# A tuned kernel's first five microseconds: which queue carries Wq's first two quarters, when the first is issued, and how many zero blocks TensorE runs

## The chip, the cores and the metric

The kernel runs on one core of a Trainium2 chip. A core has a matrix engine (TensorE, PE in the profile, its weight loads PEld), a vector engine (VectorE, DVE), a scalar engine (ScalarE, ACT), GpSimd (POOL) and SyncE (SP). SP and ACT also issue DMA transfers, each through a queue of its own; the transfers are carried out by 16 DMA engines. Each engine takes its instructions in the order in which the program gives them, and waits on semaphores for what other engines or transfers have to deliver.

The metric is the device time of one execution in microseconds (us). Beside it stands a profiled execution, whose records show every instruction and transfer.

## What is computed

The input x has 2048 rows (positions) of 512 elements, in bf16. Two branches are computed and mixed by a gate:

```python
x = A_x
g = _sigmoid((x * gate_w).sum(-1, keepdims=True))
a = _A_ref(x, A_wqkv, A_wo)
b = _B_ref(x, B_w1, B_b1, B_w2, B_b2)
return g * a + (1 - g) * b
```

Branch A projects x to q, k and v with one 512 by 1536 matrix, 32 heads of 16 each. Every position attends to eight positions, itself and the seven before it at steps of two; softmax over these eight, the weighted sum of v, and a projection with Wo. Branch B normalizes each row of x, multiplies along the positions with w1 (2048 to 1792), adds b1, applies GELU, multiplies with w2 (1792 back to 2048) and adds b2.

## The kernel before, in words

Positions are laid out in 16 tiles of 128. The kernel first needs x transposed (channels on partitions) for the projections of q and k, so the first thing it builds is the transposed x of the first 512 positions, XT, whose four blocks of 128 channels are filled in two ways. Blocks 1 to 3 come by a transposing DMA (`ld_xt0`, L473). Block 0 is loaded untransposed (`d_xp`, L479) and transposed on TensorE by four matmuls against an identity matrix (`f_tr`, L545). ScalarE (L555) and VectorE (L557) copy the results out of PSUM.

Wq, 512 by 512, is loaded in four quarters of 128 rows and 128 KB (`ld_w(0, d, 1)`), Wk in two halves of 256 KB (`ld_w(1, d, 2)`). The first projections are made for 512 positions in six groups (L635): four matmuls with Wq's first quarter and channel block 0, four with the second quarter and block 1, and so on for the third and fourth, then eight with each half of Wk. All matmuls of the projections have the line L619. The first group therefore waits for block 0 and Wq's first quarter, and the second group for the transposing DMA and Wq's second quarter.

Before the first data arrive TensorE multiplies constants into a bank that nobody reads (`f_warm`, L537): six blocks of 512 columns, one of 256, and one of 512 behind the transposes. They keep the array busy and compute nothing that is used; the text calls them zero blocks, as the change's own words do.

After the projections TensorE runs, without a gap, the scores of the attention in two bursts (L698), the two large products of branch B (L812 and L862) and the output projection (L878). VectorE makes the products of q with shifted k (L690), the row statistics of branch B (L574), the softmax, the weighted sums of v (L797 to L802) and the final mixture (L899). ScalarE copies out of PSUM (L627, L630), normalizes (L598) and applies the nonlinear functions.

The order on each engine comes from a planner in the kernel file. Operations are added with what they read and write, an estimated duration and, for the first loads, an expected landing time (`lands`); the planner places them one by one and derives semaphore waits from the data they share. Some orders are given by hand (`order.add`, `chain`). The first loads have their own waits cleared (`op_.deps.clear()`, L489), so they are issued as early as their queue allows:

```python
first_loads = [ld_w(0, 0, 1, "act"), ld_xt0(), ld_w(0, 1, 1, "act"), ld_w(0, 2, 1), ld_w(0, 3, 1), ld_w(1, 0, 2), ld_w(1, 2, 2),
               ld_x(0, 2)]
```

On SP the order of issue is: the slice for block 0, the transposing DMA, Wq's third and fourth quarter, Wk's two halves, two tiles of x, the transposing DMA of the next 512 positions, and the rest. On ACT it is Wq's first and second quarter, then a load of the activation table, then the copy at L555. GpSimd writes constants, the identity matrix (L417) and some zeros (L420, L421, L518).

Of the kernel before, what the change touches and what calls it, by code (L numbers as in the profile page):

```python
# [333 lines left out]
def bass_gated_mix__sliding_local_dilated__mixer_token_mlp__prompt_kernel(nc, A_x, A_wqkv, A_wo, B_x, B_w1, B_b1, B_w2, B_b2, gate_w, out, dbg=None):  # L334
    with contextlib.ExitStack() as es:
# [75 lines left out]
        def psub(ap_, p0, np_, offs, dims):  # L411
# [3 lines left out]
        A = sch.add  # L415

        c_ident = A("pool", lambda e: e.affine_select(out=IDENT, in_=nc.const_aps.tensor(1.0, [128, 128], BF16), pattern=[[1, 128]], compare_op=ALU.is_equal,  # L417
                                                     fill=0.0, base=0, channel_multiplier=-1),
                    0.4, writes=["ident"], name="ident")
# [8 lines left out]
        def mk_dma(dst, src):  # L428
            return lambda e: e.dma_start(dst, src)
# [3 lines left out]
        def throttle():  # L433
            return [init_dmas[-5]] if len(init_dmas) >= 5 else []

        def prev_dma():
            return [init_dmas[-1]] if init_dmas else []

        def ld_x(t0, n, q="sp"):
            ds = sch.dsem("x%d" % t0)  # L440
            op = sch.dma(q, mk_dma(X[:, t0:t0 + n, :], xv[:, t0:t0 + n, :]), n * 128 * D * 2, ds,
                         writes=["x%d" % t for t in range(t0, t0 + n)], deps=throttle() if q == "sp" else [], after=prev_dma() if q == "sp" else [], name="d_x%d" % t0)
            if q == "sp":
                init_dmas.append(op)
            return op

        def ld_w(tn, d0, n, q="sp"):
            ds = sch.dsem("wqkv%d_%d" % (tn, d0))
            op = sch.dma(q, mk_dma(WQKV[:, d0:d0 + n, tn * D:(tn + 1) * D], wqkv_v[:, d0:d0 + n, tn * D:(tn + 1) * D]),
                         n * 128 * D * 2, ds, writes=["wqkv%d_%d" % (tn, dt) for dt in range(d0, d0 + n)],  # L450
                         deps=throttle() if q == "sp" and n == 4 else [], after=prev_dma() if q == "sp" else [],
                         issue=0.65 if n == 4 else 0.45, name="d_wp%d_%d" % (tn, d0))
            if q == "sp":
                init_dmas.append(op)
            return op
# [14 lines left out]
        def ld_xt0():  # L470
            ds = sch.dsem("xt0")
            dst = XT[:, 1:4, 0:512]
            op = sch.dma("sp", lambda e: e.dma_start_transpose(dst, x2d[0:512, 128:512]), 512 * 384 * 2, ds, issue=1.25,  # L473
                         writes=XT0[1:4], after=prev_dma(), name="d_xt0")
            init_dmas.append(op)
            return op

        XP = view("OUTS", BF16, [(128, 4), (1, 128)])
        d_xp = sch.dma("sp", mk_dma(XP, xv[:, 0:4, 0:128]), 512 * 128 * 2, sch.dsem("xp"), writes=["outs0"], issue=0.4, name="d_xp")  # L479
        d_xp.lands = 3.9  # L480
        init_dmas.append(d_xp)

        first_loads = [ld_w(0, 0, 1, "act"), ld_xt0(), ld_w(0, 1, 1, "act"), ld_w(0, 2, 1), ld_w(0, 3, 1), ld_w(1, 0, 2), ld_w(1, 2, 2),
                       ld_x(0, 2)]
        ld_xt(1)
        first_loads.append(init_dmas[-1])
        for op_, t_ in zip(first_loads, (3.5, 5.7, 5.0, 6.3, 6.7, 7.6, 8.6, 9.4, 11.0)):
            op_.lands = t_
            op_.deps.clear()  # L489
        first_loads[2].order.add(first_loads[0])  # L490
        init_dmas[:] = [first_loads[1]] + first_loads[5:]
        ld_x(2, 2)
        ld_x(4, 4)
# [7 lines left out]
        def ld_w1(j):  # L501
# [4 lines left out]
            if j < 4:  # L506
# [8 lines left out]
                       writes=["wo"], deps=throttle(), after=prev_dma(), name="d_wo")  # L515
# [4 lines left out]
        for i_, (v_, n_) in enumerate(((B_b1, NFT), (B_b2, NST))):  # L520
            vr = v_.rearrange("(t q j) -> q t j", q=4, j=32)
            for q_ in range(4):
                sch.dma("sp", mk_dma(psub(BR, 32 * q_, n_, 32 * i_, [(1, 32)]), vr[q_]), n_ * 64, ds_b, reads=["br"],
                        writes=["br_%d_%d" % (i_, q_)], deps=throttle(), after=prev_dma(), name="d_b_%d_%d" % (i_, q_), issue=0.45)
        d_w1.append(ld_w1(3))
        A("dve", lambda e: e.transpose(out=BT, in_=BR), 0.2, reads=["br_%d_%d" % (i_, q_) for i_ in range(2) for q_ in range(4)],
          writes=["btc"], name="t_b")
# [5 lines left out]
        def f_warm(n, w_=D):  # L533
            def fn(e):
                ins = None
                for _ in range(n):
                    ins = e.matmul(ps[:, 7, 0:w_], lhsT=CONE[:, 0:128], rhs=CONE[:, 0:w_], start=True, stop=True)  # L537
                return ins
            return fn

        def f_tr(h):
            def fn(e):
                ins = None
                for t in range(2):
                    ins = e.matmul(ps[:, 5 + h, 128 * t:128 * t + 128], lhsT=XP[:, 2 * h + t, :], rhs=IDENT, start=True, stop=True)  # L545
                return ins
            return fn

        A("pe", f_warm(6), 2.56, writes=["lg7_0", "lg7_1"], name="warm1", prio=-100)
        w2_ = A("pe", f_warm(1, 256), 0.2, writes=["lg7_0", "lg7_1"], name="warm2", prio=-100)  # L550
        ta_ = A("pe", f_tr(0), 0.215, reads=["outs0", "ident"], writes=["lg5_0", "lg5_1"], after=[w2_], name="tr0", prio=-100)
        tr_ = A("pe", f_tr(1), 0.215, reads=["outs0", "ident"], writes=["lg6_0", "lg6_1"], after=[ta_], name="tr1", prio=-100)
        A("pe", f_warm(1), 0.43, writes=["lg7_0", "lg7_1"], after=[tr_], name="warm3", prio=-100)
# [2 lines left out]
          writes=["xt0_0"], name="ev_tra", prio=0)  # L556
        A("dve", lambda e: e.tensor_copy(out=XT[:, 0, 256:512], in_=ps[:, 6, 0:256]), 0.35, reads=["lg6_0", "lg6_1"],  # L557
          writes=["xt0_0b"], name="ev_trb", prio=0)
# [76 lines left out]
        for (b0, d0, d1, s0, s1) in ((0, 0, 1, 0, 512), (0, 1, 2, 0, 512), (0, 2, 3, 0, 512), (0, 3, 4, 0, 512), (4, 0, 2, 0, 512), (4, 2, 4, 0, 512)):  # L635
            for b in range(b0, b0 + 4):
# [3 lines left out]
                                 writes=fbn[b], after=[last_main[0]], name="pf_%s%d_%d_%d" % (tnames[tn], dl, d0, s0))  # L640
                last_main[0].order.add(w3_)
        for b, (tn, dl) in enumerate(first):
            A("act", f_evq(tn, dl, 0, b), 0.52, reads=fbn[b] + (["k5pad"] if tn == 1 else []),
              writes=["%s5_%d_0" % (tnames[tn], dl)], name="ev_%s%d_0" % (tnames[tn], dl), prio=0)
# [7 lines left out]
        for (tn, dl, sb) in seq_proj:  # L652
# [4 lines left out]
                             writes=["acc%d" % bank], after=[last_main[0]], name="pj_%s%d_%d" % (tnames[tn], dl, sb), prio=0)  # L657
            A("act", f_evq(tn, dl, sb, bank), 0.62, reads=["acc%d" % bank] + (["k5pad"] if tn == 1 else ["v5pad"] if tn == 2 else []),
              writes=["%s5_%d_%d" % (tnames[tn], dl, sb)], name="ev_%s%d_%d" % (tnames[tn], dl, sb), prio=0)
# [11 lines left out]
                writes=["xa"] + ["wqkv%d_%d" % (tn, dt) for tn in range(3) for dt in range(4)], name="d_xa")  # L671
        for t in range(NST):
# [5 lines left out]
          writes=["th"], name="g_tanh", prio=0)  # L678
# [31 lines left out]
        for wh in range(2):  # L710
# [6 lines left out]
            for (dl, c0, nc_) in pieces:  # L717
# [5 lines left out]
                  writes=wr, name="qkm_%d_%d_%d" % (wh, dl, c0), prio=0)  # L723
            rd = sum([pbn(b_) for b_ in bufs], []) + PBX[wh] + ["rp"]
            for wl in range(4):
                qop = A("pe", f_qkr(list(enumerate(bufs)), (wl,)), 0.92, reads=rd, writes=["lg%d_0" % (4 + wl), "lg%d_1" % (4 + wl)],
                        name="qkr_%d_%d" % (wh, wl), prio=-100 + wl, delay=BURST_DELAY)
                A("act", (lambda wh_, wl_: (lambda e: e.activation(out=ATT[:, :, 4 * wh_ + wl_, :], in_=ps[:, 4 + wl_, :].rearrange("p (h c) -> p h c", h=2), func=AF.Copy)))(wh, wl),  # L728
                  0.55, reads=["lg%d_0" % (4 + wl), "lg%d_1" % (4 + wl)], writes=["lw%d" % (4 * wh + wl)],
                  name="lev_%d_%d" % (wh, wl), prio=0)  # L730
# [60 lines left out]
        for k_, u in enumerate(USEQ):  # L791
# [7 lines left out]
            for (nm, n_, du) in (("ava", 4, 2.25), ("avb", 2, 1.2)):  # L799
                A("dve", (lambda pv_, n__: (lambda e: e.tensor_tensor(out=pv_[:, 0:n__], in0=pv_[:, 0:n__], in1=pv_[:, n__:2 * n__], op=ALU.add)))(pv, n_),  # L800
                  du, writes=[pn], name="%s_%d" % (nm, u))
# [27 lines left out]
        for ft in range(NFT):  # L829
# [6 lines left out]
              name="gel_%d" % ft, prio=0)  # L836
# [84 lines left out]
        for i in range(NST):  # L921
# [4 lines left out]
            elif i > 1:  # L926
# [6 lines left out]
              name="t1_%d" % i, prio=0)  # L933
# [119 lines left out]
```

## Time and profile before

| | us |
|---|---|
| median of 3 runs | 168.13 |
| lowest and highest | 168.06, 168.51 |
| the profiled execution's own time | 168.55 |
| its span | 167.3 |
| TensorE busy | 163.9 |
| VectorE busy | 151.3 |
| ScalarE busy | 75.0 |

The span runs from the first to the last instruction of the program; the profiled execution's time is 1.25 us longer than its span. Busy time counts an engine's own work, without waits and without the issue of DMAs. Since matmuls are pipelined, a matmul's recorded duration overlaps that of its neighbours, and the distance from start to start is what one costs in a row. A view of the chain lists, in order of time, the pieces of work of which each had to wait for the one before; a timeline lists instructions with their start, duration, engine, line, operation, what they write and read, and their number when several are merged; a name with q (SPq, ACTq) is the engine's sequencer, which issues transfers.

### The profile page before, as it was taken

To read this page: it belongs to the slowest core of one execution; us is meant where nothing else is said; L and a number is where in the kernel's file an instruction comes from. 1 tells how busy PE (TensorE), PEld (TensorE's weight loads), DVE (VectorE), ACT (ScalarE), POOL (GpSimd) and SP (SyncE) were. 2 spreads that over 40 slices of the span, in tenths; PEclk is the share of its full clock that TensorE was granted. 3 is DMA by queue.
4 is the path that set the end of the run, shared out by engine and by line. 5 is a ranking of instruction groups with operands and counts; after the bars stand their busy time and mean duration, and the time that the engine had idled before them with its cause. 6 is when DMAs were issued, how large, how long until landed. Compare 5 with 4: busy or idle time off the path is not lost.

```text
span 167.3 us, 2152 instructions
## 1 busy us (share of the span) xinstructions
PE 163.9 (98%) x860; PEld 77.6 (46%) x860; DVE 151.3 (90%) x154; ACT 75.0 (45%) x116; POOL 0.7 (0%) x8
## 2 busy tenths in 40 slices
PE   7999999999999999999999999999999999999994
PEld 2455555554454444444444444444444444444463
DVE  0145999999999999999999999999999999999896
ACT  3077688889899818793113121131231321310100
POOL 1000000000000000000000000000000000000000
DMA  5999999968003837996579936462672580000454
GB/s 130 315 272 262 303 322 291 307 196 246 0 0 97 311 115 187 303 290 153 133 183 343 335 129 143 112 187 68 184 218 83 138 223 0 0 0 0 157 190 159
DMA packets 47625, 29.64 MB, mean 177 GB/s; under 512 B 9856, under 2 KB 46464, under 8 KB 47616
## 3 DMA queue, kind: packets, MB, share of 16 engines
q1 hardware_dynamic: 45504, 24.85, 54.0%
q10 hardware_dynamic: 2112, 4.66, 10.0%
q8 instruction: 7, 0.11, 0.3%
q14 instruction: 2, 0.02, 0.0%
HBM read 21.24 MB, written 2.10 MB: 140 GB/s over the span
## 4 chain that ended last, share of the span: by engine, by line
PE 94%; DVE 3%; DMA 2%; issue 0%
PE ps L812 29%; PE ps L862 29%; PE ps L619 25%; PE ps L878 6%; PE ps L698 4%; DVE arena L899 2%; DMA arena<-in_A_x_dram 2%; PE ps L545 0%; DVE arena L557 0%
## 5 line engine op out<-in xcount | busy, mean ns | idle before, releaser
L812 PE MATMUL ps<-arena 128*128 128x512 bf16 x224 | 48.7, 379 | 0.0
L862 PE MATMUL ps<-arena 128*128 128x512 bf16 x224 | 48.7, 379 | 0.0
L619 PE MATMUL ps<-arena 128*128 128x512 bf16 x192 | 42.3, 382 | 0.1
L690 DVE TENSOR_TENSOR arena<-arena 128x4096 bf16<-128x4096 bf16 (+1 forms) x12 | 35.5, 2996 | 2.3 <-ACT arena L630 1.8
L797 DVE TENSOR_TENSOR arena<-arena 128x8192 bf16<-128x8192 bf16 x8 | 35.0, 4419 | 0.0
L812 PEld LDWEIGHTS ps<-arena 128*128 128x128 bf16 x224 | 21.8, 98 | 26.7 <-ACT arena L728 0.4
L862 PEld LDWEIGHTS ps<-arena 128*128 128x128 bf16 x224 | 21.9, 98 | 26.5
L619 PEld LDWEIGHTS ps<-arena 128*128 128x128 bf16 x192 | 21.6, 114 | 20.8 <-DVE arena L557 0.7
L930 ACT ACTIVATE arena<-ps,arena 128x512 bf16<-128x512 f32 x16 | 12.4, 778 | 39.4 <-PE ps L862 39.4
L800 DVE TENSOR_TENSOR arena<-arena 128x4096 bf16<-128x4096 bf16 (+1 forms) x16 | 27.0, 1752 | 0.0
L630 ACT ACTIVATE arena<-ps 128x512 bf16<-128x512 f32 x32 | 18.5, 596 | 4.5 <-PE ps L619 4.5
L833 ACT ACTIVATE arena<-ps,arena 128x512 bf16<-128x512 f32 x14 | 9.6, 687 | 22.2 <-PE ps L812 17.4
L574 DVE BATCH_NORM_STATS2 arena<-arena 128x6 f32<-128x512 bf16 x16 | 10.0, 680 | 5.6 <-DMA arena<-in_A_x_dram 5.6
L878 PE MATMUL ps<-arena 128*128 128x512 bf16 (+1 forms) x80 | 14.2, 337 | 0.0
L899 DVE SCALAR_TENSOR_TENSOR arena<-ps,arena 128x512 bf16<-128x512 f32 (+1 forms) x20 | 11.5, 638 | 0.9 <-PE ps L878 0.7
L598 ACT ACTIVATE arena<-arena 128x512 bf16<-128x512 bf16 x16 | 12.2, 806 | 0.0
L627 ACT ACTIVATE arena<-ps 128x512 bf16<-128x512 f32 x16 | 9.0, 596 | 5.5 <-PE ps L619 5.4
L878 PEld LDWEIGHTS ps<-arena 128*128 128x128 bf16 x80 | 7.8, 98 | 6.3
L674 DVE SCALAR_TENSOR_TENSOR arena<-arena 128x512 bf16<-128x512 bf16 x16 | 10.1, 685 | 0.0
L744 DVE TENSOR_TENSOR arena<-arena 128x512 bf16<-128x512 bf16 (+4 forms) x11 | 7.3, 667 | 0.6 <-ACT arena L763 0.2
L698 PE MATMUL ps<-arena 128*32 128x512 bf16 x128 | 7.3, 380 | 0.0
L728 ACT ACTIVATE arena<-ps 128x512 bf16<-128x512 f32 x8 | 4.7, 592 | 4.6 <-PE ps L698 4.6
(42 smaller groups left out, 40.5 us busy)
## 6 DMA issues: line engine op xcount, KB each, us to landing
arena<-in_B_w_dram SPq DMA_DIRECT2D x7, 1024.0 KB, 8.3
arena<-in_B_w_dram SPq DMA_DIRECT2D x8, 896.0 KB, 5.1
arena<-arena ACTq DMA_DIRECT2D x32, 128.0 KB, 3.0
arena<-in_A_x_dram SPq DMA_DIRECT2D x4, 512.0 KB, 5.1
out_dram<-arena SPq DMA_DIRECT2D x14, 128.0 KB, 1.7
arena<-in_A_x_dram SPq DMA_DIRECT2D x1, 1536.0 KB, 7.9
arena<-in_A_wqkv_dram SPq DMA_DIRECT2D x2, 256.0 KB, 3.6
arena<-in_A_x_dram SPq DMA_DIRECT2D x2, 256.0 KB, 3.5
```

What stands on the lines that cost most here:

```text
L598: A("act", (lambda t_: (lambda e: e.activation(out=X[:, t_, :], in_=X[:, t_, :], func=AF.Identity, scale=col(RSTD, t_), bias=col(NMR, t_)) ...
L619: ins = e.matmul(ps[:, bank, s0:s1], lhsT=lhsT, rhs=XT[:, dt, sb * 512 + s0:sb * 512 + s1], start=(dt == 0 and s0 == 0), stop=(dt == 3))
L630: return lambda e: e.activation(out=dst, in_=ps[:, bank, :], func=AF.Copy)
L690: return lambda e: e.tensor_tensor(out=PBL[buf][:, :, 512 * c0:512 * (c0 + nc_)], in0=in0, in1=in1, op=ALU.mult)
L698: ins = e.matmul(ps[32 * c:32 * c + 32, 4 + wl, :], lhsT=RP, rhs=PBL[buf][:, wl, c * 512:(c + 1) * 512], start=(dl == 0), stop=(dl == 3), ...
L797: A("dve", (lambda o_, i0, i1: (lambda e: e.tensor_tensor(out=o_, in0=i0, in1=i1, op=ALU.mult)))(pv, in0, in1), 4.4, reads=v_res + ["atx_% ...
L800: A("dve", (lambda pv_, n__: (lambda e: e.tensor_tensor(out=pv_[:, 0:n__], in0=pv_[:, 0:n__], in1=pv_[:, n__:2 * n__], op=ALU.add)))(pv, n ...
L812: ins = e.matmul(ps[:, bank, :], lhsT=W1W[:, slot, st, 128 * e_:128 * e_ + 128], rhs=X[:, st, :], start=(st == 0), stop=(st == NST - 1))
L862: ins = e.matmul(ps[:, bank, :], lhsT=W2S[slot][:, ft, 128 * e_:128 * e_ + 128], rhs=UT[:, ft, :], start=(ft == 0), stop=(ft == NFT - 1))
L878: ins = e.matmul(ps[:, bank, 0:c1 - c0], lhsT=OT[:, t, 128 * i:128 * i + 128], rhs=WO[:, t, c0:c1], start=(t == 0), stop=(t == 3))
L899: A("dve", (lambda i_, b_, c0_, c1_: (lambda e: e.scalar_tensor_tensor(out=T1[:, i_, c0_:c1_], in0=ps[:, b_, 0:c1_ - c0_], scalar=col(G, i ...
L930: A("act", (lambda i_, bank_: (lambda e: e.activation(out=T1[:, i_, :], in_=ps[:, bank_, :], func=AF.Identity, scale=col(OMG, i_), bias=co ...
```

## The change

Four things are edited, all in the first five microseconds.

- Wq's second quarter is issued by SP, behind the transposing DMA and ahead of the third quarter, where before it followed the first quarter on ACT.
- Wq's first quarter stays on ACT and gets a wait: it is issued once GpSimd has written the identity matrix.
- The zero block of 256 columns is gone; six of 512 remain ahead of the transposes.
- The planner's expected landing times are other numbers. The order of instructions on TensorE, VectorE, ScalarE and GpSimd is otherwise as before; on SP one issue is added, on ACT one removed.

```diff
-        d_xp.lands = 3.9
+        d_xp.lands = 3.2
 ...
-        first_loads = [ld_w(0, 0, 1, "act"), ld_xt0(), ld_w(0, 1, 1, "act"), ld_w(0, 2, 1), ld_w(0, 3, 1), ld_w(1, 0, 2), ld_w(1, 2, 2),
+        first_loads = [ld_w(0, 0, 1, "act"), ld_xt0(), ld_w(0, 1, 1), ld_w(0, 2, 1), ld_w(0, 3, 1), ld_w(1, 0, 2), ld_w(1, 2, 2),
                        ld_x(0, 2)]
 ...
-        for op_, t_ in zip(first_loads, (3.5, 5.7, 5.0, 6.3, 6.7, 7.6, 8.6, 9.4, 11.0)):
+        for op_, t_ in zip(first_loads, (3.8, 5.4, 5.7, 6.1, 6.5, 7.3, 8.1, 8.9, 10.9)):
             op_.lands = t_
             op_.deps.clear()
-        first_loads[2].order.add(first_loads[0])
+        first_loads[0].deps.add(c_ident)
 ...
-        A("pe", f_warm(6), 2.56, writes=["lg7_0", "lg7_1"], name="warm1", prio=-100)
-        w2_ = A("pe", f_warm(1, 256), 0.2, writes=["lg7_0", "lg7_1"], name="warm2", prio=-100)
+        w2_ = A("pe", f_warm(6), 2.56, writes=["lg7_0", "lg7_1"], name="warm1", prio=-100)
```

In the kernel after the change every line behind L549 has a number lower by one.

## The prediction

> **What bounds the kernel now.** I read the page first (busy shares, and the chain that ended last), then the chain in order of time, then the head, before 13 us, matmul by matmul and transfer by transfer.
>
> ```profile
> PE 163.9 (98%) x860; PEld 77.6 (46%) x860; DVE 151.3 (90%) x154; ACT 75.0 (45%) x116; POOL 0.7 (0%) x8
> ...
> PE 94%; DVE 3%; DMA 2%; issue 0%
> ...
> 0.80 3.10 DMA arena<-in_A_x_dram
> 3.91 0.14 issue
> 4.04 0.60 PE ps L545 x4
> ...
> 4.66 0.44 DVE arena L557
> 5.10 0.05 issue
> 5.15 33.44 PE ps L619 x152
> ```
>
> TensorE is the bound and never stops once it has begun the projections (L619) at 5.15 us. What lies before is one chain: the 128 KB slice of x (d_xp) issued at 0.80 lands at 3.91; four transposing matmuls run from 4.04; VectorE copies the second pair out until 5.10; the first projection starts at 5.15. So the change is worth what it does to the start of TensorE's unbroken row, minus any new gap in it.
>
> The next view is the timeline of TensorE in narrow windows: start, duration, instruction.
>
> ```profile
> 5.15 0.61 PE L619 MATMUL ps<-arena 128*128 128x512 bf16 x1
> 5.56 0.63 PE L619 MATMUL ps<-arena 128*128 128x512 bf16 x1
> 5.98 0.45 PE L619 MATMUL ps<-arena 128*128 128x512 bf16 x1
> 6.26 0.38 PE L619 MATMUL ps<-arena 128*128 128x512 bf16 x1
> 6.48 0.38 PE L619 MATMUL ps<-arena 128*128 128x512 bf16 x1
> ```
>
> Start to start is what counts: 0.41 and 0.42, then 0.28, then 0.22 (later 0.216 throughout). The array runs at half speed until about 6.12 (0.28 = 0.135 slow + half of the other 0.29) and at full speed after. The granted clock reads 1.00 in every window here, so only the spacing shows this turn. The first zero block starts at 0.84, 5.28 us ahead of it.
>
> Last, transfers and issues of the head: the timeline, and the two queues' lines for 1.9 to 3.4 us (packets, MB, share of 16 engines; q1 is SP's, q10 ACT's).
>
> ```profile
> 0.80 1.02 ACTq L429 DMA_DIRECT2D arena<-in_A_wqkv_dram  x2
> 0.80 0.43 SPq L429 DMA_DIRECT2D arena<-in_A_x_dram  x1
> ...
> 0.89 0.29 POOL L417 TENSOR_SCALAR_AFFINE_SELECT arena<-const-bfloat16-1.0 128x128 bf16<-128x128 bf16 x1 [0.38 <-POOLq L1038]
> ...
> 1.29 1.64 SPq L473 DMA_TRANSPOSE arena<-in_A_x_dram  x1
> ...
> 1.84 1.28 ACT L555 ACT_TABLE_LOAD   x1 [1.84 <-issue]
> ...
> 2.99 2.03 SPq L429 DMA_DIRECT2D arena<-in_A_wqkv_dram  x4
> ...
> q10 hardware_dynamic: 200, 0.19, 41.4%
> q1 hardware_dynamic: 523, 0.13, 38.1%
> ```
>
> While the slice moves, ACT's two quarters of Wq take more engine time than the slice itself: 41% against 38%.
>
> **The sum is made against the profiled execution**: 168.55 us, a span of 167.3 and 1.25 around it. The three runs have a median of 168.13, 0.42 less. A clock turn that comes 0.84 us earlier than this one would account for that, since each us at half speed costs half a us; the runs do not show whether that is it.
>
> **Part by part.**
>
> *First quarter of Wq, later.* It waits for GpSimd's identity, whose row ends at 1.18; the VectorE instruction with the same wait starts at 1.21, so ACT's issue moves from 0.80 to about 1.22. It landed 2.9 after issue, so now at about 4.1. The first projection needs it; its cover is the new start below (4.64), 0.5 us of slack. Queued behind the wait on ACT are the table load (1.84 to 3.12 before; now, with one issue of 0.43 ahead in place of two, about 1.68 to 2.96) and the copy at L555, which needs the transposes. Cost nothing.
>
> *The slice of x, earlier.* Until 2.6 us ACT's queue had moved 17 packets, from 2.6 to 3.0 it took 99 against the slice's 108 and 70.6% of the engines. With ACT's only load 0.42 later, those 0.4 us belong to the slice; the 256-byte packets of the next SP transfer ran alone at 1092 a us, so the slice's last 230 or so would need some 0.2 us and end near 2.9 instead of 3.4. Ends for the landing: 3.91 (nothing gained, the descriptors come no faster), and 2.5 (the shortest load-size row, a 128 KB store, lands after 1.7). I take 3.4, the 0.5 us of the packets; nearest because it is this transfer's own row. Below 3.22 it would gain nothing, as the next part shows.
>
> *Six zero blocks.* The half block (256 columns, 0.21 at half speed) goes. Blocks are 0.43 apart, so six end at 3.35, which is the earliest start of the transposes. With the slice at 3.4 plus 0.13 (3.91 to 4.04 before) they start at 3.53, 0.51 earlier. The chain behind is unchanged, 1.11 from transposes to projection: the projections start at 4.64 (ends: 4.46 and 5.15).
>
> *What of it remains.* Here the clock decides. If the turn stays at 6.12, the 0.51 us gained are spent at half speed and hold 0.51/0.427 = 1.2 matmuls, worth 1.2 x 0.216 = 0.26 at full speed. The first group of four (4.64, 5.05, 5.48, 5.90) ends at 6.22 instead of 6.48. If the turn moves along with the start, all 0.51 remains. I take the first: the removed and shifted blocks change little of the activity before the turn, all at most 0.2 us of it. [...]
>
> *Second quarter of Wq, on SP behind the transposing DMA.* It takes the slot at 2.99 that the third had, which landed 3.1 after: 6.1. It follows the transposed x, which landed at 5.7 (1.29 + 4.4) and was held up by ACT's second load, now gone: 88 packets, 45% of the engines from 3.4 to 3.9, 0.2 us. So it lands between 5.7 and 6.1, say 5.9, and the second group can start at 6.03, below 6.22: hidden in this execution. At the upper end it starts at 6.24, a loss of 0.02. With a turn as early as 5.28, the first group would end at 5.82 and the load would decide: 6.03 against 6.08 before, a gain of 0.05.
>
> *Everything behind it on SP* moves back by one issue, 0.49 at most. Fourth quarter: 3.59 + 2.9 = 6.5, then at most 7.0, needed at 7.95. Wk: 7.4 and 8.4, then 7.9 and 8.9, needed at 8.8 and 10.5. The transpose of the second 512 rows: 5.58 + 5.5 = 11.1, then 11.6, needed at 12.52 - 0.26 = 12.26. The x tiles of the statistics: 9.1, then 9.6; behind them VectorE idles 1.59 and 1.84 until ScalarE's copies release it. All covered, least by 0.65.
>
> *The rest* moves as a block: the bursts at 38.59 and 61.27 have their VectorE products 1.2 and 1.3 earlier (37.37, 59.95), and those follow the copies of the same projections.
>
> Sum: -0.26 in the profiled execution, 168.3; against the median, 168.13 less 0.05 to 0.26. I take 167.9, the turn's place unchanged.
>
> **Rivals.**
> A, the forecast: a half gain, 167.8 to 168.1. For it: the spacing above.
> B, no gain: the slice lands at 3.9 all the same, or the second quarter lands at 6.1 and the second group waits for it where the clock turns early. Then 168.0 to 168.3. For it: even alone, before 2.2 us, SP's queue moved only 62 packets in 0.3 us. [...]
> C, a full gain: the turn moves with the start, or the slice lands by 3.22; up to 0.69, so 167.4 to 167.6. For it: the array idles less before the turn (0.27 between zero blocks and transposes becomes 0.2 or less).
> D, slower, the clock: the missing half block lets the turn come later. It decides from 0.5 us of delay on, which eats the half gain; a delay of 5.3 (the whole first stretch over again) costs 2.6 less 0.26, so up to 170.5. Against it: by the rows the idle time before the turn shrinks. [...]
> E, slower, the second quarter: it lands later than 6.35 (6.48 - 0.13) and TensorE stops. The longest 128 KB load of the trace, gate_w, took 4.0: 2.99 + 4.0 + 0.13 = 7.12, so +0.64, 168.8. Against it: that one ran beside megabytes.
>
> **Chances.** A 0.57, B 0.18, C 0.12, D 0.07, E 0.06. 0.3%, 0.5 us, is about what a measurement of this kernel can tell from no change. Faster by more: C and a small tail of A, 0.16. Slower by more: most of D, half of E, 0.10. Within: 0.74. The range runs from C's end, 167.4, to 168.6, and leaves out D and most of E's far ends.
>
> **What would show it.** In the chain: d_xp lands near 3.4 and the transposes start near 3.5 (B: near 4.0). First projection near 4.6. The turn in the spacing near 6.1 (C: near 5.6; D: after 6.6). No gap ahead of the fifth projection (E: one, released by a Wq load). The prediction is wrong if the turn moves by more than 0.5 us in either direction, or if TensorE waits for a load after it has begun.

## The result and the profile after

| | before | after |
|---|---|---|
| median of 22 runs each, us | 168.28 | 168.91 |
| lowest and highest | 167.98, 169.02 | 168.20, 171.28 |
| the profiled execution's own time | 168.55 | 168.91 |

The ratio is 1.0033, with a 95% interval of 1.0021 to 1.0046: the change makes the kernel slower by a third of a per cent, some 0.55 us. The forecast was 167.9, between 167.4 and 168.6. Ratios and intervals, here and below, leave out runs more than 1.5% above the fastest of the same kernel (171.28 is one); the medians are those of all runs.

The page of the changed kernel, its busy shares and the shares of the chain that ended last:

```profile
PE 163.6 (98%) x859; PEld 77.4 (46%) x859; DVE 151.3 (90%) x154; ACT 75.0 (45%) x116; POOL 0.7 (0%) x8
...
PE 91%; DMA 3%; DVE 2%; SPq 2%; issue 0%
```

TensorE does the same work (163.6 against 163.9 us, the half block gone), but its share of the chain falls from 94% to 91%, and SP's sequencer, which was not in it, has 2%. The chain in order of time (start, us, what) says where:

```profile
0.80 0.45 SPq L429
1.25 0.06 issue
1.31 1.88 SPq L473
3.19 0.06 issue
3.24 0.57 SPq L429
3.81 0.04 issue
3.85 0.43 SPq L429
4.29 0.04 issue
4.33 0.43 SPq L429
4.76 0.04 issue
4.80 4.56 DMA arena<-in_A_wqkv_dram
9.37 0.05 issue
9.41 29.54 PE ps L618 x136
```

Before, the chain ran through the slice of x, the transposes and an unbroken row of projections from 5.15. Now it is SP's own row of issues, one behind the other: slice, transposing DMA, Wq's second, third and fourth quarter, then the first half of Wk, which lands at 9.37. Only then does TensorE's unbroken row begin. The timeline of TensorE over the first projections:

```profile
4.58 1.07 PE L618 MATMUL ps<-arena 128*128 128x512 bf16 x4
6.19 2.75 PE L618 MATMUL ps<-arena 128*128 128x512 bf16 x12 [0.55 <-DMA arena<-in_A_wqkv_dram]
9.41 4.51 PE L618 MATMUL ps<-arena 128*128 128x512 bf16 x20 [0.47 <-DMA arena<-in_A_wqkv_dram]
```

The row has two holes where it had none: ahead of the fifth projection (the second group, which reads Wq's second quarter) and ahead of the seventeenth (the first that reads Wk). From start to start, read matmul by matmul, the fourth to the fifth is 5.27 to 6.19 and the sixteenth to the seventeenth 8.57 to 9.41; less the 0.216 of a matmul, they cost 0.70 and 0.62 us.

**Where the account closes.** The thirty-third projection is the first that reads the second 512 positions, which the second transposing DMA (L460) brings. It starts at 12.52 before and at 12.89 after: 0.37 later, against 0.36 between the two profiled executions. So everything is decided by then. From 5.15 and 12.52 to 4.58 and 12.89: the start is 0.57 earlier; the slow matmuls, 0.47 us too long in all before (5.15 to 6.48 for four, less 4 x 0.216), cost 0.04, since here the clock had turned by the second projection (4.58 to 4.83); the two holes cost 1.32. -0.57 - 0.43 + 1.32 = +0.32, and 0.05 is scatter of single spacings.

This holds in nearly all of the profiles below. Own time less the start of the thirty-third projection is 156.01 to 156.13 in 18 of 20:

| profile | 5th | 17th | second transposing DMA lands | 33rd | own time | own time less 33rd |
|---|---|---|---|---|---|---|
| before | 6.48 | 9.07 | 11.04 | 12.52 | 168.55 | 156.03 |
| before, again (f1) | 6.04 | 8.63 | 11.43 | 12.08 | 168.10 | 156.02 |
| after | 6.19 | 9.41 | 12.74 | 12.89 | 168.91 | 156.02 |
| after, again (e4) | 6.40 | 9.20 | 12.50 | 12.68 | 168.81 | 156.13 |
| after without both waits for weights (h4) | 5.55 | 8.55 | 13.05 | 13.19 | 169.30 | 156.11 |

The two exceptions, 157.22 (g1) and 156.25 (g3), issue the later loads in another order; in g1 one of these stops TensorE again, as shown below. So an experiment on the head can be read at one place: what holds the thirty-third projection.

### The profile page after: what moved, and what is told of

The parts are those of the page before. It is cut to its first block, busy times and chain, and to the rows that moved or that the text cites. A ratio compares the mean times of both kernels' runs of the same rounds, so it can differ in the third digit from the quotient of the medians.

```text
span 167.6 us, 2150 instructions
## 1 busy us (share of the span) xinstructions
PE 163.6 (98%) x859; PEld 77.4 (46%) x859; DVE 151.3 (90%) x154; ACT 75.0 (45%) x116; POOL 0.7 (0%) x8
## 4 chain that ended last, share of the span: by engine, by line
PE 91%; DMA 3%; DVE 2%; SPq 2%; issue 0%
PE ps L811 29%; PE ps L861 29%; PE ps L618 23%; PE ps L877 6%; PE ps L697 4%; DMA arena<-in_A_wqkv_dram 3%; DVE arena L898 2%; SPq L429 1%; SPq L473 1%
```

## The experiments

Three theories stood in the expectations. T1: TensorE waits for Wq's second quarter, which comes too late from its new place. T2: all of SP's row behind that place is pushed back, and the loads that TensorE needs later (Wk, then the second transposing DMA) land too late. T3: the missing half block, or the later first quarter, costs the time. Times are medians of 6 to 12 runs in us; before was timed beside each, on the same chip.

### Again, and one part at a time

e4_after is the changed kernel and f1_before the kernel before, each with nothing edited, for the size of the difference and for second profiles.

> The changed kernel once more, for a second profile beside the first. T1: the second group waits near 6.2 again, the fifth does not wait or by chance. T2: the fifth group waits for Wk's first half again, by 0.3 us or more, and the half lands after 8.8. Time 168.9 in both.

> The kernel before once more, for a second profile of it. T2 in the form in which it stands now (the first thirteen microseconds are paced by the row of loads on SP, and the first profile of before was one with quick loads): at least one of Wk's first half, Wk's second half and the second transposing DMA lands over a microsecond later than in the first profile (7.44, 8.39, 11.04), and TensorE either waits for it or has less than half a microsecond left. T1 (only the second group's wait counts): the loads land as in the first profile and TensorE has no gap in its projections. Time 168.4 in both.

After: 168.93 against 168.41, 1.0035 [1.0019, 1.0051]. Before: 168.44 against 168.54, 1.0002 [0.9991, 1.0014]. The second profile of before taught more than its time. Its chain:

```profile
0.84 2.93 PE ps L537 x7
3.77 0.11 issue
3.88 0.60 PE ps L545 x4
...
4.51 0.44 DVE arena L557
...
4.99 33.15 PE ps L619 x152
```

Here the slice landed at 3.75, in time for the end of the zero blocks, and the clock had turned by the second group (fifth projection at 6.04, not 6.48). It took 168.10 us, 0.45 less than the execution that the forecast was made from: the kernel before itself spans such a difference, and the forecast's own profile was not one of the quick ones. What T2 expected of it did not come: Wk's halves and the second transposing DMA landed 0.36 to 0.62 later than in the first profile (8.06, 8.76, 11.43), not over a microsecond, and TensorE waited for none of them. In e4's profile both holes are there again, but with other shares: 1.15 us ahead of the fifth projection and 0.20 ahead of the seventeenth, where T2 had asked for 0.3 or more.

The single parts:

```diff
 e1_wq1_act, on after: the second quarter back on ACT, behind the first
-first_loads = [ld_w(0, 0, 1, "act"), ld_xt0(), ld_w(0, 1, 1), ...
+first_loads = [ld_w(0, 0, 1, "act"), ld_xt0(), ld_w(0, 1, 1, "act"), ...
+first_loads[2].order.add(first_loads[0])

 e2_wq1_sp, on before: only the second quarter's move to SP
-first_loads = [ld_w(0, 0, 1, "act"), ld_xt0(), ld_w(0, 1, 1, "act"), ...
+first_loads = [ld_w(0, 0, 1, "act"), ld_xt0(), ld_w(0, 1, 1), ...
-first_loads[2].order.add(first_loads[0])

 e3_six, on before: only the half block away
-A("pe", f_warm(6), 2.56, ...)
-w2_ = A("pe", f_warm(1, 256), 0.2, ...)
+w2_ = A("pe", f_warm(6), 2.56, ...)

 e5_ident, on before: only the first quarter's wait for the identity matrix
+first_loads[0].deps.add(c_ident)
```

> The changed kernel with one part undone: Wq's second quarter goes back to ACT behind the first, SP is as before; the wait on the identity and the six blocks stay. Theories: T1, the second group waits for Wq's second quarter, which landed at 6.06 on SP (4.31 on ACT before). T2, one more issue on SP pushes Wk's first half back (landed 9.37, before 7.44) and the fifth group waits for it. T3, the missing half block or the later first quarter costs the time through the clock or the first group. T1 and T2: the slice still lands near 3.4 to 3.6, no wait in the row of projections, second group at 6.0 or earlier, time 167.8 to 168.1 (0.2 to 0.5 under the kernel before, 168.28). T3: stays near 168.9.

> The kernel before with one part alone: Wq's second quarter on SP behind the transposing DMA, ahead of the third; the first quarter is issued at 0.80 as before, seven blocks. T1: the second group cannot start before 6.2, where it started between 6.0 and 6.5 anyway, so +0.0 to +0.2: 168.3 to 168.5. T2: Wk's first half lands after 8.6 and the fifth group waits: 168.7 to 169.0. T3: 168.3.

> The kernel before with only the half block of 256 columns taken away. T1 and T2: no change, 168.2 to 168.4, since the slice lands at 3.9 as before and the transposes wait for it. T3: slower, 168.6 to 169, with a later turn of the clock in the spacing of the projections.

> The kernel before with one part alone: ACT's first quarter waits for the identity; the second stays behind it on ACT, seven blocks. T2 in its wider form (in the head every load that comes in the way of SP's row of loads costs; at 1.63 on ACT the second quarter meets the transposing DMA): like e1, slower than the changed kernel, 169.4 to 170, with the transposing DMA landing after 6.2 and the second group waiting for it. T3 (the later first quarter as such costs through the first group): the first group waits for the first quarter, 168.8. No part in it: 168.4.

| | this | before | ratio |
|---|---|---|---|
| e1_wq1_act | 169.88 | 168.41 | 1.0073 [1.0048, 1.0097] |
| e2_wq1_sp | 168.84 | 168.41 | 1.0026 [1.0012, 1.0040] |
| e3_six | 168.33 | 168.41 | 1.0013 [0.9987, 1.0039] |
| e5_ident | 169.62 | 168.45 | 1.0096 [1.0058, 1.0133] |

The half block is worth nothing that these runs can tell (h3_after_seven, below, says so from the other side): the first half of T3 falls. The move to SP alone costs 0.26%, most of the change's 0.33%. In its profile the second group starts unhindered, and the hole is at Wk. TensorE's timeline in e2_wq1_sp:

```profile
5.09 4.20 PE L618 MATMUL ps<-arena 128*128 128x512 bf16 x16
9.56 4.29 PE L618 MATMUL ps<-arena 128*128 128x512 bf16 x19 [0.27 <-DMA arena<-in_A_wqkv_dram]
```

Sixteen projections run through (the second quarter, landed at 6.21, was used from 6.54), then the seventeenth waits for Wk's first half, which landed at 9.52, where it had landed at 7.44 and 8.06 in the two profiles of before. That speaks for T2 and against T1.

Putting the second quarter back on ACT was to cure the change, by T1 and T2 alike. It made it worse, and so did the identity's wait alone, in which the second quarter also follows the first. The chain of e1_wq1_act, from the quickest of its runs (168.76):

```profile
1.31 5.31 DMA arena<-in_A_x_dram
6.62 0.05 issue
6.66 32.14 PE ps L619 x148
```

and TensorE's timeline in e5_ident:

```profile
4.71 1.05 PE L620 MATMUL ps<-arena 128*128 128x512 bf16 x4
7.62 4.68 PE L620 MATMUL ps<-arena 128*128 128x512 bf16 x13 [1.85 <-DMA arena<-in_A_x_dram]
```

In both ACT's second load goes out at 1.63, because the first waits, where it went at 1.26 before. It then travels beside SP's transposing DMA from its start: that one needs 5.3 and 6.3 us from issue to landing in these profiles (4.4 before, 4.2 after), and the second group of projections, which reads the transposed x, waits for it. So neither theory had the reason why the load cannot stay on ACT: with the identity's wait it meets the transposing DMA there. The change's own move to SP avoids this and pays in SP's row. Its parts do not add up: 0.26% for the move, 0.96% for the wait, 0.33% for both. The 0.96% is not all this wait: six of e5's ten runs lie at 169.2 to 169.6, some 0.6% above before, and the other four 2 us higher. The profile is one of those four, and the last section shows its stretch at half clock.

### Taking the waits away

Three versions of after in which a wait has nothing to wait for. The projections in question read weights that have landed, so these kernels use other weights there; all loads are made.

```diff
 f3_no_wk_wait: in the first 512 positions, Wk's projections read Wq
-A("pe", f_proj(tn, dl, 0, b, d0, d1, s0, s1), ... reads=xt_of(0, d0, d1) + ["wqkv%d_%d" % (tn, dt) ...
+A("pe", f_proj(0, dl, 0, b, d0, d1, s0, s1), ... reads=xt_of(0, d0, d1) + ["wqkv0_%d" % dt ...

 f4_no_wq1_wait: the second group reads the first quarter in place of the second
-lhsT = sub(WQKV, dt * 3 * D + tn * D + dl, [(4, 128)])
+lhsT = sub(WQKV, (0 if (d0, d1) == (1, 2) else dt) * 3 * D + tn * D + dl, [(4, 128)])
 ... (its reads likewise)

 h4_no_waits: both
+lhsT = sub(WQKV, (0 if dt == 1 and (d0, d1) != (0, 4) else dt) * 3 * D + tn * D + dl, [(4, 128)])
+f_proj(0, dl, 0, b, d0, d1, s0, s1), ... reads ... ["wqkv0_%d" % (0 if dt == 1 else dt) ...
```

> The changed kernel, with the first 512 positions' k projections multiplied with Wq in place of Wk (that part of k is left out). All loads are as they were, but the fifth and sixth group no longer wait for Wk. T2 with Wk's first half as the place: faster, by the 0.3 to 0.8 of that wait, down to where the second transposing DMA (landed 12.50 to 12.74) stops the row: 168.5 to 168.8. T1: unchanged, 168.9.

> The changed kernel, with the second group multiplying with Wq's first quarter in place of its second (the second's part of the first projection is left out). All loads as they were; the second group waits for the transposing DMA alone. T1: faster by 0.4 to 0.8, 168.1 to 168.5. T2: the fifth group or the second transposing DMA stops the row all the same, unchanged, 168.8 to 169.0, with a longer gap there.

> The changed kernel with the first 512 positions' k multiplied with Wq and Wq's second quarter replaced by its first there (both left out), so neither the second nor the fifth and sixth group waits for its weights; all loads as they were. T2: the second transposing DMA (12.5 to 13.0) holds the row alone and nothing is gained over f3 and f4: 168.7 to 168.9. If the two waits were the cause: 168.0 to 168.4.

| | this | before | ratio |
|---|---|---|---|
| f3_no_wk_wait | 168.81 | 168.54 | 1.0020 [1.0007, 1.0033] |
| f4_no_wq1_wait | 168.88 | 168.54 | 1.0017 [1.0004, 1.0030] |
| h4_no_waits | 168.99 | 168.37 | 1.0035 [1.0019, 1.0051] |

Each single wait is worth at most a part of the loss (the intervals overlap with after's 1.0035), and both together nothing. TensorE's timeline of f4_no_wq1_wait shows why:

```profile
4.52 7.81 PE L618 MATMUL ps<-arena 128*128 128x512 bf16 x32
13.13 0.81 PE L618 MATMUL ps<-arena 128*128 128x512 bf16 x3 [0.80 <-DMA arena<-in_A_x_dram]
```

and, for the same stretch, h4_no_waits in its chain:

```profile
5.90 0.47 SPq L429
6.37 0.04 issue
6.42 6.64 DMA arena<-in_A_x_dram
13.05 0.14 issue
13.19 1.46 PE ps L618 x6
```

The first thirty-two projections get through without a long stop (the ninth waits 0.25 and 0.38 us for Wq's third quarter), and the thirty-third stands until the second transposing DMA lands, at 12.99 and 13.05. f3_no_wk_wait stops at the same place until 13.06. T1 falls as the only cause: the wait that it names can be removed, and at most a part of the time comes back. T2 holds, in its later half: three waits stand one behind the other, for Wq's second quarter, for Wk and for the second 512 positions, and all let the thirty-third projection start at about 12.7 to 13.2. In after's profile the first two decided, but the third landed only 0.15 us ahead of its use, and a start follows such a landing by 0.14 (13.05 to 13.19 in h4): without the two waits that projection would have started no more than 0.02 earlier. Take one away and the next decides.

### What fills SP's row

```diff
 f2_extra, on before: one more copy of the second quarter, 128 KB, in the place where the change issues it, into a buffer not yet in use
+def ld_dum():
+    op = sch.dma("sp", mk_dma(view("ATX", BF16, [(1, D)]), wqkv_v[:, 1, 0:D]), 128 * D * 2, ...
-ld_w(0, 1, 1, "act"), ld_w(0, 2, 1), ...
+(ld_w(0, 1, 1, "act"), ld_dum())[0], ld_w(0, 2, 1), ...

 h1_after_less on after, h2_before_less on before: 128 KB less in the row, Wq's fourth quarter (the third is read twice)
-... ld_w(0, 2, 1), ld_w(0, 3, 1), ld_w(1, 0, 2), ...
+... ld_w(0, 2, 1), ld_w(1, 0, 2), ...
 ... (weights and reads of the fourth quarter become those of the third)

 h3_after_seven, on after: the half block back
-w2_ = A("pe", f_warm(6), 2.56, ...)
+A("pe", f_warm(6), 2.56, ...)
+w2_ = A("pe", f_warm(1, 256), 0.2, ...)
```

> The kernel before with one load more on SP: a second copy of Wq's second quarter, 128 KB, into a buffer that is free until 15 us, in the place where the change puts the quarter; the quarter itself still comes on ACT. Nothing waits for the copy before VectorE's product at some 25 us. T1: the second group's wait is not there, so 168.3 to 168.5. T2: everything behind it on SP is pushed back as in the changed kernel, so 168.7 to 169.1.

> The changed kernel without the load of Wq's fourth quarter (its 128 rows are left out: every use multiplies with the third quarter's in their place). SP's row then has as many issues and bytes ahead of Wk and the second transposing DMA as before; the second group still waits for Wq's second quarter on SP. T2 (128 KB more in a row that is already full): back to the kernel before or a little under, 168.1 to 168.5. T1 (the second group's wait alone): unchanged, 168.8 to 169.0.

> The kernel before without the load of Wq's fourth quarter (its rows left out in the same way), so with 128 KB less on SP than before. T2, if the row of loads holds the kernel before too: 167.9 to 168.3. If before is held by TensorE's own start and clock, as the prediction had it: 168.3 to 168.5, no change.

> The changed kernel with the half block of zeros put back. It ends at 3.56 in place of 3.35 and the slice is there at 3.3 to 3.4, so transposes and first projection come 0.1 later. T2: no change, 168.9, since the loads decide. T3 (the half block's absence costs, now that the slice is early): back to 168.4.

| | this | before | ratio |
|---|---|---|---|
| f2_extra | 168.90 | 168.54 | 1.0023 [1.0010, 1.0036] |
| h1_after_less | 168.70 | 168.37 | 1.0018 [1.0004, 1.0032] |
| h2_before_less | 168.09 | 168.37 | 0.9979 [0.9965, 0.9994] |
| h3_after_seven | 168.79 | 168.37 | 1.0025 [1.0008, 1.0043] |

f2_extra leaves ACT, the first quarter, the zero blocks and every data dependence of before as they are, and only puts 128 KB into SP's row. TensorE's timeline in it:

```profile
5.09 3.64 PE L625 MATMUL ps<-arena 128*128 128x512 bf16 x16 [0.29 <-DVE arena L563]
8.91 3.65 PE L625 MATMUL ps<-arena 128*128 128x512 bf16 x16 [0.18 <-DMA arena<-in_A_wqkv_dram]
12.72 1.24 PE L625 MATMUL ps<-arena 128*128 128x512 bf16 x5 [0.16 <-DMA arena<-in_A_x_dram]
```

The row stops at the seventeenth and at the thirty-third projection, for Wk's first half and the second transposing DMA, and the time is that of e2_wq1_sp. This is T2 by itself: one issue and 128 KB more in that place cost 0.23% (f2) and 0.26% (e2), whether or not a projection waits for them. The two parts, the issue and the bytes, are not told apart by these runs. The converse holds for before, which gains 0.2% from one load less: one of its twelve runs lies above 168.25, against 23 of before's 35. In after the same removal leaves 0.18%, more than T2 expected (168.1 to 168.5) and less than T1 did (168.8 to 169.0): its row stops at the second group until 6.79 (second quarter landed at 6.65) and no more behind it. So with the row relieved, T1's wait is what remains.

Why the row has no room is seen in before's windows (window, length, busy us of TensorE, weight loads, VectorE, ScalarE and GpSimd, granted clock, share of the 16 DMA engines, GB/s):

```profile
4.00:6.00 2.00, 1.87 (x8) 0.76 (x9) 0.42 (x1) 0.38 (x1) 0.00 (x0) 1.00 1.17 305
6.00:8.00 2.00, 2.00 (x11) 1.04 (x10) 0.00 (x0) 0.00 (x0) 0.00 (x0) 1.00 1.06 313
```

The DMA engines are full (1.06 and more; packets overlap) at 305 to 313 GB/s; at that rate 128 KB more take 0.42 us of all of them, an estimate. Over the first 4 us they are not: the share is 0.48 in before and 0.57 in f1_before. ACT's second load, issued at 1.26, uses some of that room; on SP it goes out at 3.24. By 4 us the two profiles of before have moved 0.50 and 0.53 MB, those of after 0.44 and 0.48 (e4_after). The two queues draw on the same 16 engines: from 3.0 to 3.4 us in before, ACT's takes 54% of them and SP's 65%. But the place of issue also sets the time of issue, 1.26 on ACT and 3.24 on SP, and so whether a load meets engines with room or full ones.

The same windows of after:

```profile
4.00:6.00 2.00, 1.55 (x6) 0.38 (x4) 0.42 (x1) 0.27 (x1) 0.00 (x0) 1.00 1.03 235
6.00:8.00 2.00, 1.81 (x9) 1.01 (x10) 0.00 (x0) 0.00 (x0) 0.00 (x0) 1.00 0.97 245
```

Nearly as full, but only 235 to 245 GB/s: a byte holds an engine for longer (16 engines times the share over the rate is 0.070 and 0.063 ns, against 0.061 and 0.054 in before), though the windows do not hold the same transfers. Over 2 to 12 us the profiles of before move 278 and 267 GB/s (f1), those of after 235 and 237 (e4). That comes on top of the 128 KB, and it is not the order alone: e3_six, with the order of loads of before, moved 234 in its profile, and its second transposing DMA landed at 12.70. What makes the packets slower in one execution than in another is open.

### Moving what is late, and starting earlier

g1, g2 and g3 issue the second transposing DMA ahead of the two tiles of x that the statistics read: g1 on after, g2 on before, g3 on f3_no_wk_wait.

```diff
 ... (ld_xt returns its op)
-               ld_x(0, 2)]
-ld_xt(1)
-first_loads.append(init_dmas[-1])
+               ld_xt(1)]
+first_loads.append(ld_x(0, 2))
```

> The changed kernel with one exchange on SP: the first two x tiles for the statistics (256 KB) go behind the second transposing DMA, which is issued one place earlier. T2 (the row of loads on SP decides, through whichever load TensorE meets late, at the last the second transposing DMA, at 12.5 to 13.0): the transposing DMA lands 0.5 to 1 earlier; what remains is Wk's first half, so 168.6 to 168.9, a gain of 0.0 to 0.3. If the transposing DMA alone decides: 168.3 to 168.5. T1: unchanged, 168.9.

> The kernel before with the same exchange. T2: the second transposing DMA lands 0.5 to 1 earlier there too; it stopped TensorE in one of three profiles of that order (e3, 1.0 us), so the median gains 0.0 to 0.2 and the upper runs go: 168.2 to 168.4. T1: unchanged, 168.4. Slower if the statistics' tiles now come late for VectorE.

> f3 (the changed kernel, k of the first 512 positions multiplied with Wq, that part of k left out, so no wait for Wk) with the exchange of g1. T2: both of the late places are relieved and the second group's start near 6.3 decides: 168.2 to 168.5, 0.3 to 0.6 under f3 (168.81). If the second group's wait were the cause: no change against f3.

| | this | before | ratio |
|---|---|---|---|
| g1_x0_behind_after | 169.73 | 168.45 | 1.0069 [1.0049, 1.0089] |
| g2_x0_behind_before | 168.52 | 168.45 | 1.0004 [0.9986, 1.0021] |
| g3_x0_behind_no_wk | 168.83 | 168.45 | 1.0025 [1.0009, 1.0041] |

Both expectations of T2 on after were missed, and the one on before too (g2 gained nothing; T1 had expected that). In g1 the second transposing DMA did land earlier, at 11.57, and the thirty-third projection started at 12.44; but a later transposing DMA is then late, and TensorE's timeline has a new hole:

```profile
17.83 2.54 PE L618 MATMUL ps<-arena 128*128 128x512 bf16 x11
21.41 1.89 PE L618 MATMUL ps<-arena 128*128 128x512 bf16 x8 [1.04 <-DMA arena<-in_A_x_dram]
```

In g3 the second 512 positions are there at 12.20, ahead of need, and the second group decides: it waits for Wq's second quarter until 6.62, and from there the row is unbroken. No change against f3 is what was expected if that wait were the cause: where the loads behind no longer stop the row, it alone costs 0.25% here and 0.18% in h1. This is the third time that a wait taken away uncovers another.

v1 and v2 try for a better kernel: ACT issues the slice of x ahead of Wq's first quarter, so that SP starts at 0.80 with the transposing DMA and its whole row is earlier by one issue. v1 is on after, without the wait for the identity; v2 is on before, which has no such line.

```diff
-d_xp = sch.dma("sp", mk_dma(XP, xv[:, 0:4, 0:128]), ...
+d_xp = sch.dma("act", mk_dma(XP, xv[:, 0:4, 0:128]), ...
-init_dmas.append(d_xp)
-first_loads[0].deps.add(c_ident)
+first_loads[0].order.add(d_xp)
```

> A version built on the finding that SP's row of loads paces the head: the slice of x goes to ACT, ahead of Wq's first quarter (0.80 and about 1.25), so that SP begins with the transposing DMA at 0.80 and every load behind it is issued 0.5 earlier than in the changed kernel; second quarter on SP, six blocks. T2: the transposing DMA lands near 5.1, the second one 0.3 to 0.5 earlier than in the changed kernel, so 168.3 to 168.6, and no better than before if the slice is held up by the transposing DMA (3.9 or later). T1: the second quarter lands 0.5 earlier, 168.4.

> The same exchange made in the kernel before: ACT issues the slice, the first and the second quarter, SP begins with the transposing DMA and has the fewest loads of all versions; seven blocks. T2: 167.9 to 168.2 if the second quarter, issued at 1.7 on ACT, does not meet the transposing DMA as in e1 and e5; 169 or more if it does (that DMA would land after 6.0).

v1: 168.44 against 168.34, 1.0008 [0.9983, 1.0033]. v2: 168.72 against 168.34, 1.0029 [1.0003, 1.0054]. The chain of v1:

```profile
0.80 0.46 ACTq L429
1.25 0.03 issue
1.28 3.35 DMA arena<-in_A_wqkv_dram
4.63 0.09 issue
4.72 33.44 PE ps L616 x152
```

With the second quarter still on SP, but the row earlier (it lands at 5.55, Wk's first half at 7.67, the second transposing DMA at 11.52), the projections run unbroken from 4.72, and the loss of the change cannot be seen any more, though the interval still reaches the change's 1.0033. No gain over before shows either. In v2 the first projection waits for Wq's first quarter until 5.67, as ACT has three loads in a row; the transposing DMA landed at 5.80, and 168.72 lies in neither of the two expected ranges. No version that computes the whole result beat the kernel before.

## Why the prediction was wrong

**Right: the slice, the transposes, the first projection, the zero blocks.** The slice landed at 3.34 (said: 3.4), the transposes started at 3.47 (3.53), the first projection at 4.58 (4.64), the first quarter landed at 3.92 (4.1, needed by then). The half block costs nothing that e3_six and h3_after_seven can tell. The gain at the start was there in full, 0.57 us.

**Wrong, and decisive: "Everything behind it on SP moves back by one issue, 0.49 at most ... All covered, least by 0.65".** The step priced the moved load in the time of its issue and took the landing times of one profile. In that one the clock turned late and the loads came quickly. Wk's first half was to land by 7.9 and landed at 9.37; the second transposing DMA by 11.6, needed at 12.26, and landed at 12.74. For the latter the two terms can be read apart. The issues of that transposing DMA, in SP's timeline, before:

```profile
5.58 3.25 SPq L460 DMA_TRANSPOSE arena<-in_A_x_dram  x1
```

and after:

```profile
6.30 4.37 SPq L460 DMA_TRANSPOSE arena<-in_A_x_dram  x1
```

It is issued 0.72 later, not by at most 0.49 (Wq's second quarter itself goes out at 3.24, not at 2.99, as the first transposing DMA's issue lasted 1.88 instead of 1.64), and from issue to landing it takes 6.43 instead of 5.46, 0.97 more. The step had the first term at two thirds and the second at nothing; and its margin of 0.65 left out the time from landing to start, 0.14 in h4. f1_before's profile, had it been the one at hand, would have left little room: 11.43 landed, and wanted before 12.08.

**The second quarter's own landing** was right at the edge of its range: 6.06 after (said 5.7 to 6.1), 6.26 in e4, 6.46 and 6.65 in h3 and h1. In after TensorE stopped for it, 0.70 us in this profile, because the clock had turned early. That is the case that the text gave as a gain of 0.05, "with a turn as early as 5.28": the price was against 6.08 in before, and the load would have had to land at 5.9. So "hidden in this execution" failed too, and not in this profile alone. In the seven profiles of after and its variants with the second quarter on SP in which the wait remains (after, e4, f3, g1, g3, h1, h3) the fifth projection starts at 6.19 to 6.79, with a median of 6.40; in the six with Wq's first two quarters on ACT as before (before, f1, e3, f2, g2, h2) it is 5.84 to 6.48, with a median of 6.02. What the first projection gained is lost again four projections later. It is also rival E's place. But one load late by itself is not the whole cause: without that wait the kernel is still 0.17% slower than before (f4_no_wq1_wait), and without it and Wk's, 0.35% (h4_no_waits).

**The turn of the clock**, forecast as unchanged (6.12), moved. By the spacing of the matmuls, zero blocks included, it lies near 4.7 in after, 5.4 in f1_before, 3.5 in e4 and 6.3 in e2. So rival C's condition, a turn that moves, was met in after's profile, and its gain was there: 0.43 us of slow matmuls fewer. It bought nothing, because the row then ran into the loads sooner. The forecast asked whether the start's gain survives the clock; what it did not survive was the next wait. What sets the turn no run here shows: with nothing edited it lay at 6.1 in one execution of before and at 5.4 in the other.

Of rival B, the slice at 3.9 did not occur, but its second reason did: the second quarter landed at 6.1, and the second group waited for it after an early turn. Its price, no gain, left out the loads behind. Rival D did not occur. Both signs that the text gave of being wrong came: the turn moved by more than 0.5 us, and TensorE waited for loads after it had begun. Slower had a chance of 0.10, from the clock and the second quarter; the missing rival was a shift of the whole row of loads, with its deciding point at the landing of the second transposing DMA, some 12.26.

**What stays open.** Why the same loads move 235 GB/s in some executions and 278 in others, with the engines as full; how much of after's loss belongs to the load more in SP's row (f2_extra and e2_wq1_sp: 0.23 and 0.26%) and how much to the second quarter's wait (g3 and h1: 0.25 and 0.18%), since either alone comes near the whole and their intervals overlap with that of after; and whether before gains from h2's relief because it, too, has executions with a late transposing DMA, which e3_six's profile suggests.

## What to carry to other kernels

A load that is put ahead of others in a full queue can cost all that follow more than its issue (here 0.72 us in the issue and 0.97 from issue to landing), and it is not free because its own deadline holds: list the deadline of every load behind it, against landings of more than one profile. Where a row of work waits at several loads in turn, find the first instruction after which the kernel's end is a constant away (here the thirty-third projection), and price the change there. Early, idle time of the transfer engines is worth keeping: the load that went out at 1.26 us stopped nothing in before, and on SP, 2 us later, it cost 0.26% (e2_wq1_sp).

## What the runs showed of the hardware

- A plain 128 KB load issued by ACT at 1.63, just behind SP's transposing DMA (1.3), made that one need 5.3 (e1) and 6.3 us (e5) from issue to landing, against 4.0 to 4.4 in seven profiles with that load at 1.26 or on SP's own queue (before, f1, e3; after, e4, f4, h4).
- The issue of the second transposing DMA (512 rows) holds SP's sequencer for 3.25 (before) to 4.57 us (h4); SP's next issue follows 0.04 to 0.05 us behind its end (before, f1, e3, after, e4, f4, e1, e5).
- A stop of TensorE of 2.0 us was followed by half its clock. In e5's profile the projections started at 5.39 and 7.62 enclose the stop, and soon behind it TensorE ran at half speed for 3.4 us (columns as in the windows above; the granted clock is the last but two):

```profile
4.46:7.86 3.40, 1.43 (x6) 0.53 (x6) 0.20 (x1) 0.00 (x0) 0.00 (x0) 1.00 1.17 199
7.86:11.28 3.42, 3.42 (x10) 1.20 (x9) 0.80 (x2) 0.00 (x0) 0.00 (x0) 0.50 1.16 321
11.28:14.00 2.72, 2.72 (x14) 1.47 (x13) 0.82 (x2) 2.07 (x4) 0.00 (x0) 1.00 0.94 270
```

  The 3.42 us at 0.50 cost 1.7, half of them, an estimate, and e5's times fall into two groups, 169.2 to 169.6 and 171.3 to 171.8. The profiled execution, 171.41, is of the upper group; that the others of it ran such a stretch at half clock too is not shown. TensorE was busy for 1.43 of the 3.40 us ahead of the slow stretch. After stops of 1.2 us (e1, e4) the row went on at full speed: in e1 the 148 matmuls behind the stop take 32.14 us, 0.217 each, and in e4 the granted clock is 1.00 in every window from 2 to 12 us.
- The turn to full speed at the start (in before matmuls 0.41 to 0.43 us apart, then 0.216, while the granted clock reads 1.00 throughout) came anywhere from 3.5 to 6.3 us in these profiles, at different times also between two executions of one kernel (f1 and before: 5.4 and 6.1).
